# Attention and a gated feed-forward on one core: masks and residual additions moved from GpSimd to VectorE, output matmuls given a later priority

## The chip, the cores and the metric

The kernel runs on one core of a Trainium2 chip. The metric is device time in microseconds of one execution, the median of the runs made. A core has five engines that run their own instruction queues in order: TensorE (PE in the rows, its weight loads PEld), VectorE (DVE), ScalarE (ACT), GpSimd (POOL) and SyncE (SP). They meet only through semaphores.

## The reference

Four batches of eight heads, 768 positions, 64 channels each. Heads 0, 2 and 6 attend causally to everything; the other five see the first four positions and a window of 64. The 3072 tokens that come out, 512 wide, pass a gated feed-forward with hidden width 1536:

```python
scores = scale * np.matmul(q, k.transpose(0, 1, 3, 2))
stream_keep = causal & (is_sink | in_win)
full_mask = np.broadcast_to(causal, (H, S, S))
mask = np.where(retr[0, :, 0, 0, None, None], full_mask, stream_mask)
scores = np.where(mask[None, :, :, :], scores, -1000000000.0)
a = np.exp(scores)
a = a / (np.sum(a, axis=-1, keepdims=True) + 1e-09)
x = np.matmul(a, v)
...
g = x @ w_gate
gelu = 0.5 * g * (1.0 + erf(g * inv_sqrt2))
val = x @ w_val
ffn_out = gelu * val @ w_out
res_gate = 1.0 / (1.0 + np.exp(-(x @ w_res)))
return x + res_gate * ffn_out
```

## The kernel before

The program is a graph of tasks. Each task names its engine, a guessed duration, the tasks whose data it needs (`deps`), tasks that it merely has to follow (`order`), a priority (`prio`, lower is earlier) and the buffers it uses. `schedule()` plays the graph through once when the kernel is built: whenever an engine is free it takes, among its tasks that are ready and whose buffers are to be had, the one of lowest priority number. Tasks made with `flex` may go to one of several engines, whichever ends first by the guessed durations plus `BIAS`. What comes out is a fixed instruction order for each engine, with semaphore waits added. So a priority decides the order, and nothing is decided at run time.

The tokens come in six chunks of four tiles of 128 (`CHUNKS`); chunks 1 and 4 join two half tiles of two batches and so work with 256 query columns where the others have 512. A chunk c goes through four parts.

- *Loads and transposes.* GpSimd's queue issues the loads of q, k and v (L444) into two staging buffers `qks`. In chunks 0 and 1 TensorE transposes q and k (L524) at priority 1000c - 550; later chunks use transposing DMAs on SP.
- *Attention*, priority 1000c to 1000c + 200: per pair of heads the scores (L621), `exp` on ScalarE (L633) into `er` (causal heads) or `es` (the others), a multiplication by a 0/1 mask (L661; VectorE or GpSimd), the values matmul (L689), whose 65th column gives the sum, a reciprocal (L696) and the normalisation (L699) on VectorE into `xtok`. For every two heads a cast to fp16 (L713; VectorE, ScalarE or GpSimd), TensorE transposes (L719) and copies out of PSUM into `xT` (L726; VectorE or ScalarE).
- *Gate and value*, priority 1000c + 500: for each of twelve blocks of 128 hidden units four gate and four value matmuls of 512 columns (L763), GELU on ScalarE (L770), product on VectorE into `hT` (L772).
- *Outputs*, priority 1000c + 1600: for each of four token tiles four residual-gate matmuls (L788, weights `wr`), twelve output matmuls (L793, weights `wo`), a tanh on ScalarE (L796), the gated product on VectorE (L798), the addition of `xtok` (L801; on GpSimd, in the last chunk on VectorE) and the store through SP (L807).

By these priorities the outputs of chunk c - 1 run among the attention of chunk c: scores and values first, output matmuls where TensorE would wait. The scores of a chunk are held until the gate matmul of the eleventh block of the chunk before (`near_end`). Eight PSUM banks serve all this: two for the values matmuls, six for the rest, of which the feed-forward may hold five (`moe`) and scores and transposes four (`scr`).

Of the kernel before, what the change touches and what calls it, by code (L numbers as in the profile page):

```python
# [38 lines left out]

class Task:  # L40
    __slots__ = ("eng", "dur", "fn", "deps", "order", "prio", "bufs", "fset", "dma",
                 "ndeps", "users", "ready", "end", "done", "pos", "snap", "waits",
                 "signal", "name", "sem", "seq", "grp", "alts")

    def __init__(self, eng, dur, fn, deps, prio, bufs=(), fset=None, dma=0.0, order=(), name="", grp=None):
# [58 lines left out]
BIAS = {"act": 0.2, "dve": 0.5, "pool": 0.0}  # L104
# [254 lines left out]
def build_kernel(nc, q, k, v, w_gate, w_val, w_out, w_res, out):  # L359
# [27 lines left out]
    P_ot = Pool(many("otile", 3, [128, D_MODEL], FP32))  # L387
# [3 lines left out]
    P_ps = Pool(banks[2:8], caps={"moe": 5, "scr": 4})  # L391
# [104 lines left out]
    def loads_rows(c, si, b, a, z):  # L496
# [20 lines left out]
        for p in ORDER:  # L517
            pr = 1000 * c - 550 + p if c else 40 * ORDER.index(p) - 5
# [42 lines left out]
    last_gelu = {-1: None}  # L561
    chunk_xt = {-1: []}
    near_end, last_sc, exps_of = {}, {}, {}

    def attention(c, lt0, b, a, z, xbuf, xtbuf, xtoks, xttoks):
# [3 lines left out]
        for k_, p in enumerate(ORDER):  # L569
            pr = 1000 * c + 40 * k_ + (80 if lt0 else 0)  # L570
            side = []
            for h in PAIRS[p]:
# [4 lines left out]
                else:  # L577
# [14 lines left out]
    def scores(c, BB, p, pr, sides, r):  # L592
# [37 lines left out]
    def exps(c, pr, S_, blocks, scr, ts):  # L630
# [9 lines left out]
        while i < len(blocks):  # L640
# [23 lines left out]
            tm = G.flex({"dve": (c_dve(w * 128, 1.4, False), fm), "pool": (c_pool(w * 128, 0.55), fm)}, [tx, mt], pr,  # L664
# [43 lines left out]
    def to_features(c, lt0, n, cb, pr, normed, xbuf, xtbuf, xttoks):  # L708
        x16 = Buf(P_x16)
        def cast(on):  # L710
            def fn(e):
# [172 lines left out]
```

## Time and profile before

| | us |
|---|---|
| runs | 305.07, 309.48, 305.82 |
| median | 305.82 |
| profiled execution | 304.34 |
| its span (first to last instruction) | 302.3 |
| TensorE busy | 279.0 |
| ScalarE busy | 162.1 |
| VectorE busy | 143.3 |
| GpSimd busy | 136.8 |
| mean granted clock of TensorE | 0.989 |

The trace is of one execution. Busy time of an engine counts its computing instructions; issuing a DMA shows as busy on GpSimd's row where its duration is told. The window view gives each engine's busy time in a stretch and the share of full clock that TensorE was granted there; the timeline gives instructions with the idle time just before them and what ended it, in square brackets; the chain follows the work that ended last back to its releasers.

### The profile page before, as it was taken

Reading aid. Unit: us, or ns where it says so; the run is one execution under the profiler, and the core shown is the slowest. Engines: PE = TensorE matmul, PEld = TensorE weight load, DVE = VectorE, ACT = ScalarE, POOL = GpSimd, SP = SyncE. Lnnn points to the kernel's source line nnn. Section 1 sums busy time; section 2 is a strip of 40 time slices with the busy share of each in tenths; the row PEclk is TensorE's granted clock in tenths of the full one; section 3 lists DMA queues with packets and bytes.
Section 4 is the critical chain, followed back from the end, with each engine's and each line's share of the span. In section 5 each row is a group of like instructions: output and inputs, shape, how many; then the busy total and the mean of one; then the engine's idle time right before and its main releaser. Section 6 shows DMA issues by size and latency. Waiting matters only on the chain.

```text
span 302.3 us, 5444 instructions
## 1 busy us (share of the span) xinstructions
PE 279.0 (92%) x2162; PEld 136.3 (45%) x2162; DVE 143.3 (47%) x332; ACT 162.1 (54%) x305; POOL 136.8 (45%) x179
## 2 busy tenths in 40 slices
PE   5986799998489999989999999999999999989994
PEld 5653344454234435534445444445444345444441
DVE  6564334368734324743446443237843315633333
ACT  2896444766143577743376733565643667743310
POOL 8999099686948356680016300347700025400000
PEclk9999999999699999999999999999999999999999
DMA  8999999999999978999301100010100001000011
GB/s 88 184 198 204 174 201 194 158 150 139 153 192 204 104 78 85 85 161 174 61 1 40 67 2 0 18 54 15 58 35 2 0 35 37 37 35 0 2 70 69
DMA packets 92265, 26.94 MB, mean 89 GB/s; under 512 B 81152, under 2 KB 88912, under 8 KB 92240
## 3 DMA queue, kind: packets, MB, share of 16 engines
q0 software_dynamic: 70320, 14.69, 57.9%
q1 hardware_dynamic: 21920, 11.91, 19.3%
q8 instruction: 17, 0.28, 0.4%
q14 instruction: 8, 0.07, 0.1%
HBM read 29.36 MB, written 6.29 MB: 118 GB/s over the span
## 4 chain that ended last, share of the span: by engine, by line
PE 81%; DMA 6%; DVE 5%; POOL 5%; ACT 1%; issue 1%; POOLq 0%; DVEq 0%
PE pb L763 38%; PE pb L793 21%; PE pb L621 7%; PE pb L788 7%; DMA qks<-in_q_dram 6%; PE pb L689 4%; PE pb L719 2%; DVE es L661 1%; POOL va L444 1%; ACT xT L726 1%; POOL qks L444 1%; DVE x L713 1%; DVE xtok L699 1%; PE pb L524 1%; POOL wg L444 1%
## 5 line engine op out<-in xcount | busy, mean ns | idle before, releaser
L763 PE MATMUL pb<-xT,wg 128*128 128x512 f16 x288 | 86.3, 381 | 3.5 <-ACT xT L726 2.5
L772 DVE SCALAR_TENSOR_TENSOR hT<-gact,pb 128x512 f16<-128x512 f16 x72 | 49.5, 687 | 77.2 <-ACT gact L770 77.2
L763 PE MATMUL pb<-xT,wv 128*128 128x512 f16 x288 | 85.6, 383 | 0.2 <-DMA wv<-in_moe_w_val_dram 0.2
L770 ACT ACTIVATE gact<-pb 128x512 f16<-128x512 f32 x72 | 43.0, 597 | 68.8 <-PE pb L763 68.8
L793 PE MATMUL pb<-wo,hT 128*128 128x512 f16 x288 | 73.2, 380 | 0.0
L801 POOL TENSOR_TENSOR otile<-otile,xtok 128x512 f32<-128x512 f32 x20 | 25.4, 1273 | 67.9 <-DVE otile L798 65.4
L763 PEld LDWEIGHTS pb<-xT,wv 128*128 128x128 f16 x288 | 27.8, 98 | 33.2 <-issue 0.6
L763 PEld LDWEIGHTS pb<-xT,wg 128*128 128x128 f16 x288 | 26.3, 98 | 35.0 <-ACT xT L726 4.6
L633 ACT ACTIVATE er<-pb 128x512 f16<-128x512 f32 (+2 forms) x72 | 34.9, 548 | 9.4 <-PE pb L621 9.3
L633 ACT ACTIVATE es<-pb 128x512 f16<-128x512 f32 (+1 forms) x60 | 31.0, 568 | 10.9 <-PE pb L621 9.4
L793 PEld LDWEIGHTS pb<-wo,hT 128*128 128x128 f16 x288 | 23.9, 97 | 25.2 <-issue 2.1
L444 POOL DMA_DIRECT2D qks<-in_k_dram x36 | 28.4, 816 | 13.4 <-PE pb L524 8.6
L798 DVE SCALAR_TENSOR_TENSOR otile<-srs,pb 128x512 f32<-128x512 f32 x24 | 16.4, 684 | 32.6 <-PE pb L793 22.7
L621 PE MATMUL pb<-qkt 64*128 64x128 f16 (+6 forms) x416 | 30.1, 244 | 0.0
L444 POOL DMA_DIRECT2D qks<-in_q_dram x36 | 28.4, 820 | 0.3 <-POOL ident L415 0.3
L661 POOL TENSOR_TENSOR es<-es,m_diag 128x256 f16<-128x256 f16 (+1 forms) x14 | 11.9, 858 | 29.8 <-ACT es L633 29.8
L788 PE MATMUL pb<-wr,xT 128*128 128x512 f16 x96 | 24.7, 380 | 0.0
L444 POOL DMA_DIRECT2D va<-in_v_dram x24 | 21.5, 933 | 5.2 <-PE pb L689 5.2
L621 PEld LDWEIGHTS pb<-qkt 64*128 64x128 f16 (+1 forms) x416 | 13.9, 97 | 18.2 <-issue 6.2
L699 DVE TENSOR_TENSOR xtok<-pb,rcp 128x256 f32<-128x256 f32 (+1 forms) x64 | 21.4, 350 | 0.7
L696 DVE RECIPROCAL rcp<-pb 128x4 f32<-128x4 f32 (+1 forms) x64 | 10.6, 172 | 23.6 <-PE pb L689 22.7
L796 ACT ACTIVATE srs<-pb 128x512 f32<-128x512 f32 x24 | 14.3, 599 | 10.1 <-PE pb L788 10.1
(52 smaller groups left out, 243.7 us busy)
## 6 DMA issues: line engine op xcount, KB each, us to landing
out_dram<-otile SPq DMA_DIRECT2D x24, 256.0 KB, 2.0
va<-in_v_dram POOLq DMA_DIRECT2D x24, 128.0 KB, 12.0
qks<-in_k_dram POOLq DMA_DIRECT2D x32, 64.0 KB, 10.6
qks<-in_q_dram POOLq DMA_DIRECT2D x32, 64.0 KB, 10.7
wg<-in_moe_w_gate_dram POOLq DMA_DIRECT2D x3, 512.0 KB, 11.8
wv<-in_moe_w_val_dram POOLq DMA_DIRECT2D x3, 512.0 KB, 13.6
wo<-in_moe_w_out_dram POOLq DMA_DIRECT2D x4, 384.0 KB, 24.9
qks<-in_q_dram POOLq DMA_DIRECT2D x4, 256.0 KB, 11.7
```

Of the source, the lines that this page charges most:

```text
L444: return G.add(eng, issue, lambda e: e.dma_start(out_ap(), in_ap), deps, prio, bufs=bufs, dma=cost, name=name, grp=grp)
L621: return [e.matmul(at(scr)[rows, o:o + nq * 128], lhsT=at(BB.qkt)[half, 1, kt, p, ks], rhs=at(BB.qkt)[half, 0, q0:q0 + nq, p, :], start=Tr ...
L633: tx = G.add("act", c_act(cols), lambda e: e.activation(out=at(et)[:, off:off + cols], in_=at(scr)[:, 0:cols], func=AF.Exp, scale=SM_SCALE ...
L661: fm = lambda e, o0=off + o, w=w, msk=msk: e.tensor_tensor(out=at(et)[:, o0:o0 + w * 128].rearrange("p (i k) -> p i k", k=128), in0=at(et) ...
L699: t2 = G.add("dve", c_dve(n * 64), lambda e: e.tensor_tensor(out=at(xbuf)[:, lt0:lt0 + n, h * 64:(h + 1) * 64], in0=at(av)[:, 0:n * 65].re ...
L763: return lambda e: [e.matmul(at(dst)[:, :], lhsT=w[:, ci, f * 128:(f + 1) * 128], rhs=at(xtbuf)[:, ci, :], start=(ci == 0), stop=(ci == NC ...
L770: ta = G.add("act", c_act(512), (lambda gb=gb, ga=ga: lambda e: e.activation(out=at(ga)[:, :], in_=at(gb)[:, :], func=AF.Gelu))(), [tg], p ...
L772: th = G.add("dve", c_dve(512), (lambda vb=vb, ga=ga, f=f: lambda e: e.scalar_tensor_tensor(out=at(h)[:, f, :], in0=at(ga)[:, :], scalar=0 ...
L788: e.matmul(at(rb)[:, :], lhsT=at(xtbuf)[:, ci, s], rhs=wr[:, ci, :], start=(ci == 0), stop=(ci == NCB - 1))
L793: e.matmul(at(fb)[:, :], lhsT=at(h)[:, fi, s], rhs=wo[:, fi, :], start=(fi == 0), stop=(fi == NF - 1))
L798: t1 = G.add("dve", c_dve(512), (lambda fb=fb, sr=sr, ot=ot: lambda e: e.scalar_tensor_tensor(out=at(ot)[:, :], in0=at(sr)[:, :], scalar=1 ...
L801: fa = lambda e, ot=ot, lt=lt: e.tensor_tensor(out=at(ot)[:, :], in0=at(ot)[:, :], in1=at(xbuf)[:, lt, :], op=ALU.add)
```

## The change

Masks are `add`ed on VectorE alone; casts choose between VectorE and ScalarE; the residual additions are on VectorE in every chunk, at a priority 90 behind the rest of their token tile. So GpSimd computes nothing after the constants and only issues loads. `BIAS` is lowered by 0.2 for ScalarE and 0.3 for VectorE. The transposes of q and k of chunk 1 get a priority of 1000c - 492, which is behind the first eight gate blocks of chunk 0 instead of ahead of all. The outputs go from 1000c + 1600 to 1000c + 2400, behind the gate and value matmuls of the next chunk; but the first half of these (those of the first two channel blocks) is set to 1000c + 1499 until all feature copies of the chunk are done. The residual-gate matmuls must now follow the last value matmul of their chunk. `xtok`, `xT` and `otile` get one buffer more each, and the feed-forward may hold four PSUM banks instead of five. The orderings between chunks are the same ones, gathered in a loop at the end; `SPLIT` is empty, so the branches for part "A" do nothing.

```diff
-BIAS = {"act": 0.2, "dve": 0.5, "pool": 0.0}
+BIAS = {"act": 0.0, "dve": 0.2}
...
                 for t in cand[e]:
+                    if t.boost and all(x.end is not None and x.end <= now for x in t.boost[0]):
+                        t.prio, t.boost = t.boost[1], None
...
-    P_x = Pool(many("xtok", 2, [128, 4, D_MODEL], FP32))
+    P_x = Pool(many("xtok", 3, [128, 4, D_MODEL], FP32))
-    P_xt = Pool(many("xT", 2, [128, NCB, 512], FP16))
+    P_xt = Pool(many("xT", 3, [128, NCB, 512], FP16))
-    P_ot = Pool(many("otile", 3, [128, D_MODEL], FP32))
+    P_ot = Pool(many("otile", 4, [128, D_MODEL], FP32))
-    P_ps = Pool(banks[2:8], caps={"moe": 5, "scr": 4})
+    P_ps = Pool(banks[2:8], caps={"moe": 4, "scr": 4})
...
-            pr = 1000 * c - 550 + p if c else 40 * ORDER.index(p) - 5
+            pr = 1000 * c - 492 + p if c else 40 * ORDER.index(p) - 5
...
-            tm = G.flex({"dve": (c_dve(w * 128, 1.4, False), fm), "pool": (c_pool(w * 128, 0.55), fm)}, [tx, mt], pr,
+            tm = G.add("dve", c_dve(w * 128, 1.4, False), fm, [tx, mt], pr,
                         bufs=[et], name=f"mask{S_.h}")
...
-        tc_ = G.flex({"dve": (c_dve(n * 128, 1.2, False), cast("dve")), "act": (c_act(n * 128), cast("act")),
-                      "pool": (c_pool(n * 128), cast("pool"))},
+        tc_ = G.flex({"dve": (c_dve(n * 128, 1.2, False), cast("dve")), "act": (c_act(n * 128), cast("act"))},
...
+                if c0 == 0 and c > 0:
+                    for t in (tg, tv):
+                        t.boost, t.prio = ([t_ for _, t_ in xttoks], pr), 1000 * c + 1499
...
-            pr = 1000 * c + 1600 + 10 * lt
+            pr = 1000 * c + 2400 + 10 * lt
...
-                for ci in range(NCB)])(), [t for _, t in xttoks] + [wtok["r"]], pr, bufs=[rb, xtbuf], name="res")
+                for ci in range(NCB)])(), [t for _, t in xttoks] + [wtok["r"]], pr, bufs=[rb, xtbuf],
+                       order=[ph(c, "gv")[-1][1]], name="res")
...
-            alts = {"dve": (0.69, fa)} if c == len(CHUNKS) - 1 else {"pool": (1.3, fa)}
-            t2 = G.flex(alts, [t1] + xtoks[lt], pr, bufs=[ot, xbuf], name="add")
+            t2 = G.add("dve", 0.69, fa, [t1] + xtoks[lt], pr + (0 if c == len(CHUNKS) - 1 else 90), bufs=[ot, xbuf], name="add")
...
+    for c in range(len(CHUNKS)):
+        gv, gelu = ph(c, "gv"), ph(c, "gelu")
+        for f, t in gv:
+            t.order += ph(c, "scA") + ph(c, "scB")
...
+        for t in ph(c + 1, "scB"):
+            t.order += [x for f, x in gv if f == NF - 2] + ph(c, "xT")
+        for t in ph(c + 1, "expB"):
+            t.order += gelu[NF - 1:]
```

The first place is GpSimd during the attention of chunk 1. Before, masks, a cast and additions stand between the loads of q (`in_q_dram`), k and v:

```order
L661 TENSOR_TENSOR es<-es,m_diag 128x256
L661 TENSOR_TENSOR es<-es,m_prev 128x256
L444 DMA qks<-in_k_dram 128x4x64
L713 CAST x<-xtok 128x256
L444 DMA qks<-in_q_dram 128x4x64 x2
L444 DMA qks<-in_k_dram 128x4x64 x2
L444 DMA qks<-in_q_dram 128x4x64 x2
L661 TENSOR_TENSOR es<-es,m_prev 128x128 x2
L444 DMA va<-in_v_dram 128x8x64 x4
L661 TENSOR_TENSOR es<-es,m_diag 128x256
L661 TENSOR_TENSOR es<-es,m_prev 128x128
L801 TENSOR_TENSOR otile<-otile,xtok 128x512 x3
```

Now, at the same loads, nothing but loads:

```order
L451 DMA qks<-in_k_dram 128x4x64 x2
L451 DMA va<-in_v_dram 128x8x64 x4
L451 DMA qks<-in_q_dram 128x4x64 x2
L451 DMA qks<-in_k_dram 128x4x64 x2
L451 DMA qks<-in_q_dram 128x4x64 x2
```

The computing instructions have gone from the queue, and so has everything that a load had to wait behind other than a free buffer.

The second place is VectorE at the end of the attention of chunk 1, up to the first hidden-layer product. Before, with `m_prev`, `m_diag` and `m_causal` the masks, `rcp` the reciprocals:

```order
L661 TENSOR_TENSOR es<-es,m_prev 128x128
L661 TENSOR_TENSOR er<-er,m_causal 128x256
L661 TENSOR_TENSOR es<-es,m_prev 128x128
L696 RECIPROCAL rcp<-pb 128x2
L661 TENSOR_TENSOR es<-es,m_diag 128x256
L699 TENSOR_TENSOR xtok<-pb,rcp 128x2x64
L696 RECIPROCAL rcp<-pb 128x2
L699 TENSOR_TENSOR xtok<-pb,rcp 128x2x64
L696 RECIPROCAL rcp<-pb 128x2
L699 TENSOR_TENSOR xtok<-pb,rcp 128x2x64
L696 RECIPROCAL rcp<-pb 128x2
L699 TENSOR_TENSOR xtok<-pb,rcp 128x2x64
```

Now (L673 is the mask, L708 the reciprocal, L711 the normalisation, L725 the cast, L815 the gated product, L818 the addition in the changed file):

```order
L673 TENSOR_TENSOR es<-es,m_diag 128x256
L673 TENSOR_TENSOR es<-es,m_prev 128x128
L673 TENSOR_TENSOR es<-es,m_diag 128x256
L673 TENSOR_TENSOR es<-es,m_prev 128x128
L708 RECIPROCAL rcp<-pb 128x2
L815 SCALAR_TENSOR_TENSOR otile<-srs,pb 128x512
L711 TENSOR_TENSOR xtok<-pb,rcp 128x2x64
L708 RECIPROCAL rcp<-pb 128x2
L725 CAST x<-xtok 128x256
L711 TENSOR_TENSOR xtok<-pb,rcp 128x2x64
L815 SCALAR_TENSOR_TENSOR otile<-srs,pb 128x512 x2
L818 TENSOR_TENSOR otile<-otile,xtok 128x512 x3
```

Four masks stand together, three gated products and a cast stand among the last reciprocals and normalisations, and three additions follow at the end, behind all attention work of the chunk. Chunk 4 has the same rows in the changed kernel.

The third place is TensorE in the gate and value stretch of chunk 0. Before, the transposes of chunk 1's q and k (L524) begin after 28 gate and value matmuls:

```order
L763 MATMUL pb<-xT,wv 128x512 x2
L763 MATMUL pb<-xT,wg 128x512 x2
L763 MATMUL pb<-xT,wv 128x512 x2
L524 MATMUL pb<-ident,qks 64x128 x12
L763 MATMUL pb<-xT,wg 128x512 x2
L524 MATMUL pb<-ident,qks 64x128 x4
L763 MATMUL pb<-xT,wv 128x512 x2
L524 MATMUL pb<-ident,qks 64x128 x16
L763 MATMUL pb<-xT,wg 128x512 x2
```

Now they come later, sixteen at a time, each sixteen behind a pair of gate and value blocks (L776 is the gate and value matmul, L531 the transpose in the changed file):

```order
L776 MATMUL pb<-xT,wv 128x512 x2
L776 MATMUL pb<-xT,wg 128x512 x2
L776 MATMUL pb<-xT,wv 128x512 x2
L531 MATMUL pb<-ident,qks 64x128 x16
L776 MATMUL pb<-xT,wg 128x512 x2
L776 MATMUL pb<-xT,wv 128x512 x2
L776 MATMUL pb<-xT,wg 128x512 x2
L776 MATMUL pb<-xT,wv 128x512 x2
L531 MATMUL pb<-ident,qks 64x128 x16
```

Ahead of the first of these transposes stand 64 gate and value matmuls of chunk 0 instead of 28, ahead of the last sixteen 88 instead of 40.

## Rows read from the trace of the kernel before

**Rows 1.** Page, part 1: span, then busy time, share and instructions of each engine.
```profile
span 302.3 us, 5444 instructions
PE 279.0 (92%) x2162; PEld 136.3 (45%) x2162; DVE 143.3 (47%) x332; ACT 162.1 (54%) x305; POOL 136.8 (45%) x179
```

**Rows 2.** Windows: length, busy PE, PEld, DVE, ACT, POOL (count), PEclk, DMA, GB/s.
```profile
51.70:84.67 32.97, 27.01 (x240) 13.11 (x241) 20.15 (x61) 19.33 (x40) 26.53 (x36) 0.90 1.96 151
103.84:131.57 27.73, 26.35 (x256) 12.92 (x257) 13.13 (x36) 20.77 (x39) 18.39 (x23) 1.00 0.84 88
150.31:171.14 20.83, 20.43 (x203) 10.41 (x203) 11.53 (x30) 16.10 (x32) 8.29 (x9) 1.00 0.07 26
190.53:218.67 28.14, 27.49 (x253) 13.68 (x251) 16.47 (x54) 17.88 (x36) 16.87 (x24) 1.00 0.10 39
238.04:265.64 27.60, 26.28 (x257) 12.91 (x257) 12.19 (x32) 20.28 (x38) 10.24 (x9) 1.00 0.08 30
```

**Rows 3.** Chain that ended last: start us, us, what; 86 gate and value matmuls.
```profile
219.31 18.73 PE pb L763 x86
```

**Rows 4.** Windows at chunk 1's end, columns as in rows 2.
```profile
74.50:80.10 5.60, 0.86 (x8) 0.28 (x9) 5.57 (x7) 0.77 (x2) 5.60 (x7) 0.74 1.96 154
80.10:84.70 4.60, 3.65 (x17) 1.49 (x18) 1.18 (x5) 1.60 (x4) 4.60 (x7) 0.57 1.69 159
```

**Rows 5.** Timeline there: start us, us, engine, line, what [idle before <-releaser].
```profile
75.58 2.88 DVE L661 TENSOR_TENSOR es<-es,m_prev 128x128 f16<-128x128 f16 x1
...
75.91 3.69 POOL L801 TENSOR_TENSOR otile<-otile,xtok 128x512 f32<-128x512 f32 x3
...
80.09 0.21 PE L689 MATMUL pb<-va,es 128*128 128x65 f16 x1 [3.68 <-DVE rcp L696]
...
82.08 1.06 PE L763 MATMUL pb<-xT,wv 128*128 128x512 f16 x2
```

**Rows 6.** VectorE durations: timeline, groups (busy us, mean ns), one line (ns min/median/max).
```profile
66.39 0.28 DVE L661 TENSOR_TENSOR es<-es,m_diag 128x256 f16<-128x256 f16 x1
...
210.50 0.21 DVE L661 TENSOR_TENSOR es<-es,m_prev 128x128 f16<-128x128 f16 x1
...
L696 DVE RECIPROCAL rcp<-pb 128x2 f32<-128x2 f32 x32 | 5.0, 166 | 11.0 <-PE pb L689 10.6
L699 DVE TENSOR_TENSOR xtok<-pb,rcp 128x128 f32<-128x128 f32 x32 | 8.7, 285 | 0.3
L798 DVE SCALAR_TENSOR_TENSOR otile<-srs,pb 128x512 f32<-128x512 f32 x24 | 16.4, 684 | 32.6 <-PE pb L793 22.7 <-ACT srs L796 9.7
L801 DVE TENSOR_TENSOR otile<-otile,xtok 128x512 f32<-128x512 f32 x4 | 2.8, 692 | 0.1
L713 DVE CAST x<-xtok 128x256 f16<-128x256 f32 x4 | 2.8, 702 | 0.0
L726 DVE COPY xT<-pb 128x256 f16<-128x256 f16 x5 | 1.4, 285 | 0.7 <-PE pb L719 0.5
...
L713 DVE CAST x<-xtok x5: 395/565/1052, 71.7 to 217.4; 128x256 f16<-128x256 f32 x4, 128x512 f16<-128x512 f32 x1
```

**Rows 7.** Chunk 0's gate stretch: timeline of PE, then rows of the chain.
```profile
27.51 0.60 PE L763 MATMUL pb<-xT,wg 128*128 128x512 f16 x2 [0.69 <-ACT xT L726]
...
33.46 0.53 PE L524 MATMUL pb<-ident,qks 128*64 128x128 f16 x12 [1.89 <-DMA qks<-in_q_dram]
...
15.47 17.94 DMA qks<-in_q_dram
...
38.92 0.57 PE pb L524 x16
```

**Rows 8.** wo's loads (issue ns, first and last start; median landing), first output matmul.
```profile
L444 POOL DMA_DIRECT2D wo<-in_moe_w_out_dram x4: 860/872/888, 23.1 to 25.4; - x4
...
wo<-in_moe_w_out_dram POOLq DMA_DIRECT2D x4, 384.0 KB, 24.9
...
L793 PE MATMUL pb<-wo,hT x288: 377/379/390, 53.0 to 297.8; 128*128 128x512 f16 x144
```

More of the change, by code (lines that the diff above doesn't have):

```diff
@@ L37 @@
 ROWS_UNTIL = 2
+SPLIT = {c: (6, ((0, 0), (1, 0), (2, 0), (3, 0)) if len(CHUNKS[c]) > 1 else ((0, 0), (2, 0))) for c in ()}
 class Task:
@@ L51, in __init__ @@
         self.ready = 0.0
+        self.end = None
         self.done = None
@@ L57, in __init__ @@
         self.alts = None
+        self.boost = None
 class Buf:
@@ L559, in loads_natural, with ph, part @@
                 values(b, a, z, base, False)
-    last_gelu = {-1: None}
-    chunk_xt = {-1: []}
-    near_end, last_sc, exps_of = {}, {}, {}
+    phase = {}
+    def ph(c, part):
+        return phase.setdefault((c, part), [])
+    def part(c, p, late):
+        return "A" if c in SPLIT and (p, late) in SPLIT[c][1] else "B"
     def attention(c, lt0, b, a, z, xbuf, xtbuf, xtoks, xttoks):
@@ L581, in attention @@
                     h, Buf(P_er if IS_RETRIEVAL[h] else P_es), pack(diag, rest), {}, {}, 0
+                S_.part = part(c, p, int(lt0 > 0))
                 side.append(S_)
@@ L623, in sc @@
                     for (_, _, half, scr, rows, (kt, ks), o, q0, nq) in mms]
-        ts = G.add("pe", c_mm(128, dur), sc, deps, pr, bufs=scrs + [BB.qkt], order=chunk_xt[c - 1] + [near_end.get(c - 1)],
-                   name=f"sc{p}")
-        last_sc.setdefault(c, []).append(ts)
+        ts = G.add("pe", c_mm(128, dur), sc, deps, pr, bufs=scrs + [BB.qkt], name=f"sc{p}")
+        ph(c, "sc" + S_.part).append(ts)
         for (x, S_), scr in zip(sides, scrs):
@@ L755, in gate_value @@
         toks = []
-        G.add("act", 0.2, lambda e: e.activation(out=scratch[:, :], in_=ident[:, 0:1], func=AF.Gelu), [t_ident],
-              1000 * c - 100, fset="gelu", order=exps_of[c], name="table")
+        for part_ in ("B", "A") if c + 1 in SPLIT else ("B",):
+            ph(c, "table" + part_).append(G.add(
+                "act", 0.2, lambda e: e.activation(out=scratch[:, :], in_=ident[:, 0:1], func=AF.Gelu), [t_ident],
+                1000 * c - 100 + (600 if part_ == "A" else 0), fset="gelu", name="table"))
         for f in range(NF):
@@ L827, in build_kernel @@
         output(c, h, htoks, xbuf, xtoks, xtbuf, xttoks)
+    for c in range(len(CHUNKS)):
+        gv, gelu = ph(c, "gv"), ph(c, "gelu")
+        for f, t in gv:
+            t.order += ph(c, "scA") + ph(c, "scB")
+        for t in ph(c, "tableB"):
+            t.order += ph(c, "expA") + ph(c, "expB")
+        if c + 1 == len(CHUNKS):
+            continue
+        m = SPLIT[c + 1][0] if c + 1 in SPLIT else NF
+        for t in ph(c + 1, "scB"):
+            t.order += [x for f, x in gv if f == NF - 2] + ph(c, "xT")
+        for t in ph(c + 1, "expB"):
+            t.order += gelu[NF - 1:]
+        for t in ph(c + 1, "scA"):
+            t.order += [x for f, x in gv if f == m - 2] + ph(c, "xT")
+        for t in ph(c + 1, "expA"):
+            t.order += gelu[m - 1:m]
+        for t in ph(c, "tableA"):
+            t.order += ph(c + 1, "expA")
+        for f, t in gv:
+            if f >= m:
+                t.order += ph(c + 1, "scA")
+        for f in range(m, NF):
+            gelu[f].order += ph(c + 1, "expA")
     span = G.schedule()
```

18 lines of the change are left out of this document (9 added, 9 removed).

## Prediction

> **What bounds the kernel now.** Read the page's engine line first [rows 1]: TensorE is busy 279.0 of 302.3 us, no other engine above 162, so the end is set by TensorE, and a change can win only where TensorE waits, or lose by making it wait. The profiled execution took 304.34 us, 2.04 more than its span; the three timed runs have a median of 305.82. I sum changes against the profiled execution and put them on the median, which is what will be compared.
>
> Next comes the table by stretch [rows 2]: the five stretches in which attention of chunk 1 to 5 runs with the outputs of the chunk before, each from the end of the gate matmuls before it to the first gate matmul that no attention work interrupts. Subtract TensorE's busy time from each length. Chunks 2 to 5 leave 1.4, 0.4, 0.7 and 1.3 us idle. Chunk 1 leaves 6.0 idle, and its granted clock is 0.90. Chunks 1 and 4 have the same tiles, so they are each other's yardstick: chunk 4 took 28.14, of which about 2.6 are twelve output matmuls that stand only here, ahead of its first score (12 times the 0.218 of [rows 3], 18.73 us for 86), hence 25.5. Chunk 1 took 32.97, that is 7.4 more for the same work.
>
> Where those 7.4 go is seen at chunk 1's end [rows 4, 5]. From 74.5 to 80.1 TensorE is busy 0.86 of 5.6 us, while VectorE and GpSimd are both busy throughout. A VectorE mask of 128x128 takes 2.88 us; such a mask takes 0.21 elsewhere [rows 6]. Beside it run three GpSimd residual additions, 3.69 us, and it ends when they are nearly done. The values matmul behind it starts at 80.09 after 3.68 idle. After this pause the clock is granted at 0.57 up to 84.7, and a pair of 512-column matmuls takes 1.06 us instead of 0.60 [rows 7]: the array is partly at 1.2 instead of 2.4 GHz.
>
> The other large wait is in chunk 0's gate and value stretch [rows 7]: the transposes of chunk 1's q and k stand in TensorE's order ahead of the data. TensorE idles 1.89 us at 33.46 for the q load, which landed after a 17.94 us transfer. The first score of chunk 1 is at 51.70 [rows 2].
>
> **The change, step by step.** Read from the order of instructions, since the planner decides it.
>
> *Chunk 0's stretch.* The first q and k transposes now stand behind 64 gate and value matmuls instead of 28, eight of these ahead of the stretch and 56 in it. From 27.51 to 51.70 are 24.2 us; the work in it is 86 of 96 gate and value matmuls (18.7 us) and 64 transposes in four times about 0.55 (2.2), 20.9 in all, so 3.3 are waits. In the changed order 88 matmuls are left (19.2), with the transposes 21.4; these start 56 times 0.218, or 12.2 us, after the stretch begins, about 39, when the old kernel ran its last transposes unhindered (38.92). Also the last two feature copies, which ScalarE made one after the other so that TensorE idled 0.69 at 27.51, are now split between ScalarE and VectorE: the stretch starts some 0.6 sooner, about 26.9. I add 0.4 for PSUM banks, as each new block of 16 transposes needs four at once. The first score then comes at 26.9 + 21.4 + 0.4 = 48.7: **-3.0**. Bounds: -2.0 (1 us more of bank waits) to -3.6.
>
> *Chunk 1.* GpSimd has no additions, masks or casts left; the collision of [rows 5] cannot occur, and the stretch becomes that of chunk 4, whose new order it shares row by row. Its price is therefore that of chunk 4 after the change.
>
> *Chunk 4.* VectorE receives 14 masks, four additions and three casts here. Counting its new instructions in the stretch and multiplying by [rows 6]: 21 masks of 256 columns at 0.28, five of 128 at 0.21, 16 reciprocals at 0.166, 16 normalisations at 0.285, four gated products at 0.684, four additions at 0.692, five casts at 0.702, three copies at 0.285: 24.0 us, where it was busy 16.5 of 28.14. If none of this reaches TensorE the stretch can lose at most its idle time, -0.7; if all that is added does, +7.5. What decides is the end: four masks now stand as a block right ahead of the last two heads' values matmuls, 0.98 us, and a gated product between the last reciprocal and its normalisation, which chunk 4 had before too. Against that, the masks meet no GpSimd work any more. Nearest is the old chunk 4, with work of the same kind: I take **+0.5**, hence 25.5 + 0.5 = 26.0 for both, and for chunk 1 32.97 - 26.0 = **-6.9** (bounds -7.4 to 0).
>
> Casts may still collide with the issue of loads, which stays on GpSimd: five VectorE casts of before took 395 to 1052 ns, the widest of them the shortest [rows 6]. If each of five in the stretch were held for one whole issue of 0.87 [rows 8], 4.4 us, of which 0.3 each is in the 0.702 already, VectorE would have 2.9 more to do; that is part of the second rival. [...]
>
> *Chunk 3.* Only here are output matmuls really held back: the last twelve move from behind the gate stretch to between the last values matmuls and the last transposes, where they cover normalisation and cast. TensorE idles 0.4 in this stretch: **-0.3** (bounds -0.4 to +1.0, if masks queue on VectorE).
>
> *Chunks 2 and 5.* The last transposes and the first gate matmuls keep nearly their order, and the chain from the last values matmul over VectorE, cast and copy stays: **0** each (-0.7 to +1.5). The additions now stand ahead of the hidden-layer products of the next stretch; four take 2.8 us [rows 6], while GELU has still to give the first product its input, and what the products feed are output matmuls that come behind all gate matmuls, 18.7 us [rows 3]. One fewer PSUM bank for the feed-forward is covered: two feature blocks alternate over four banks, a bank is needed again two blocks later.
>
> *Loads.* Queued alone, they start when staging is free. Chunk 1's transposes end near 48 instead of 39.5 [rows 7], so chunk 2's loads start some 8 us later, but chunk 2's scores are 45 us away then, and a load took 18. The tail behind the last gate matmul keeps its order. Both at 0.
>
> Sum: -3.0 - 6.9 + 0.5 - 0.3 = -9.7; 305.82 - 9.7 = **296.1**, and a profiled execution of about 294.6.
>
> **Rivals.**
> 1. *As above*, with each term near its value: 292 to 299.5, **62 in 100**.
> 2. *VectorE becomes the bound of chunks 1 and 4.* For it: 24.0 us of instructions against 25.5 us, in order, with reciprocals that wait for TensorE between them. Against: consecutive instructions overlap a little, and in old chunk 4 masks met GpSimd's, so that part of its 16.5 was waiting. With half of the 7.5 on the path in both, 3.8 instead of 0.5 each, and 0.7 more in chunks 2, 3 and 5: -9.7 + 6.6 + 2.1 = -1.0, so 304.8. **15 in 100.**
> 3. *The slower side: the clock falls at the end of chunks 1 and 4.* If VectorE's block of masks, gated product and casts leaves TensorE a pause like the 3.68 us of [rows 5], the clock follows and both stretches cost what chunk 1 cost: no gain in chunk 1, +7.4 in chunk 4: -3.0 + 7.4 - 0.3 = +4.1, or 309.9. It decides from a pause of that length on; I count at most about 1.5 us in one piece (0.98 of masks, and a cast with its latency). **6 in 100.** The Trainium skill, "TensorE: Matmul & The Clock Gate" (What's actually happening), calls the slow clock the default, which activity lifts; the 0.57 behind the pause agrees.
> 4. *Chunk 0's gain is given back.* TensorE reaches the first output matmul, at 53.0 before, 3 us sooner; the last of its four weight loads is issued at 25.4, and the four land 24.9 later in the median, so near 50.3 or somewhat after [rows 8]. If all of the first term is lost there, 299.1. Against: that quarter is wanted by the last three of twelve matmuls only, 2 us behind the first, and loads may land sooner where GpSimd does nothing else. **11 in 100.**
> 5. *More than forecast*, if chunk 4 also loses its idle time and chunks 2 and 5 some of theirs: -9.7 - 2.4 = -12.1, 293.7 or less; below 292 **6 in 100.**
>
> **How the numbers follow.** The likeliest case gives 296.1. The range leaves out case 3, half of case 2 and most of what is below 292: 292 to 303.5. About 2% (6.1 us, to 299.7) is what a measurement of this kernel can tell from no change. Faster by more: case 1, case 5 and a little of case 4, **0.69**; within: most of 2 and 4, part of 3, **0.26**; slower (over 311.9): **0.05**.
>
> **What would show it.** First score of chunk 1 near 48.7 and no TensorE wait for a q load; chunk 1's stretch near 26 with clock 1.00; no mask over 0.5 us; chunk 4's near 26. Wrong if TensorE's waits there end on VectorE masks, or the clock dips in either.

## Result, and the profile after

| | before | after |
|---|---|---|
| median of the runs, us | 306.47 | 296.47 |
| ratio to before | | 0.965, 95% interval 0.9554 to 0.9746 |
| profiled execution, us | 304.34 | 295.47 |
| its span, us | 302.3 | 293.6 |

Timed again on another chip beside two other kernels (below), the changed kernel took 298.46 against 306.27, a ratio of 0.9725 (0.9667 to 0.9784). Executions more than 1.5% above the fastest of their kernel are left out of the ratios. The change is worth 8 to 10 us.

The page's engine line of the changed kernel, to be held against [rows 1]:

```profile
span 293.6 us, 5444 instructions
PE 278.1 (95%) x2162; PEld 137.6 (47%) x2162; DVE 152.3 (52%) x393; ACT 160.0 (55%) x301; POOL 86.5 (29%) x122
```

TensorE's busy time hardly moved (279.0 to 278.1): what went is its waiting. VectorE has 61 instructions more and is busy 9 us longer, GpSimd 57 fewer and 50 us less.

From here on "chunk c takes" means the time from the last gate or value matmul of chunk c - 1 to that of chunk c, so that the same work is counted whatever the order in it. One row is one chunk, from 0 to 5; columns as in [rows 2]. Before:

```profile
0.00:51.53 51.53, 42.13 (x456) 24.46 (x456) 25.19 (x54) 29.17 (x60) 41.89 (x64) 1.00 1.42 178
51.53:103.68 52.15, 46.19 (x329) 21.73 (x328) 28.32 (x73) 26.30 (x52) 36.56 (x48) 0.93 1.93 164
103.68:150.15 46.47, 45.09 (x343) 21.34 (x342) 20.69 (x47) 27.73 (x51) 22.17 (x26) 1.00 1.06 105
150.15:190.37 40.22, 39.77 (x292) 19.00 (x292) 19.09 (x41) 23.66 (x44) 9.02 (x9) 1.00 0.06 21
190.37:237.88 47.51, 46.82 (x341) 22.21 (x339) 24.03 (x65) 25.22 (x49) 16.87 (x24) 1.00 0.08 29
237.88:284.22 46.34, 45.02 (x344) 21.43 (x344) 19.75 (x43) 27.25 (x50) 10.24 (x9) 1.00 0.06 24
```

After:

```profile
0.00:48.57 48.57, 42.96 (x456) 25.73 (x456) 25.18 (x55) 28.41 (x59) 29.84 (x49) 1.00 1.41 181
48.57:94.61 46.04, 44.66 (x329) 21.16 (x328) 25.86 (x86) 25.55 (x50) 33.51 (x45) 1.00 2.03 158
94.61:140.92 46.31, 44.82 (x343) 21.42 (x342) 23.18 (x52) 27.32 (x50) 23.15 (x30) 1.00 1.52 140
140.92:183.21 42.29, 42.23 (x303) 20.50 (x302) 23.04 (x53) 23.13 (x43) 0.00 (x0) 1.00 0.07 26
183.21:229.25 46.04, 44.66 (x329) 21.12 (x328) 25.70 (x86) 25.55 (x50) 0.00 (x0) 1.00 0.06 24
229.25:275.56 46.31, 44.82 (x344) 21.52 (x344) 23.18 (x52) 27.32 (x50) 0.00 (x0) 1.00 0.06 24
```

The first column of numbers is the length. Chunk 0 ends 2.96 us sooner; chunk 1 takes 6.11 less, at a granted clock of 1.00 instead of 0.93; chunk 2, 0.16 less. Twelve output matmuls (2.59 us, by 12 times 0.216) moved from chunk 4's row into chunk 3's; without them chunk 3 takes 0.5 less and chunk 4 1.1 more. Chunk 5 and the tail stay. That is the whole difference of the spans, 8.7.

Chunk 4's end after the change, where [rows 5] showed chunk 1's end before; start, us, engine, line, what, and in brackets the idle time before and what ended it (chunk 1's end has the same rows, with idle times of 0.78, 0.17 and 0.36 too). The names of the lines are those of the changed file: L673 mask, L701 values, L711 normalisation, L725 cast, L730 transpose, L815 gated product.

```profile
206.50 0.28 DVE L673 TENSOR_TENSOR es<-es,m_diag 128x256 f16<-128x256 f16 x1
...
206.84 0.20 PE L701 MATMUL pb<-va,es 128*128 128x65 f16 x1 [0.78 <-DVE es L673]
...
207.33 0.67 DVE L815 SCALAR_TENSOR_TENSOR otile<-srs,pb 128x512 f32<-128x512 f32 x1
207.92 0.28 DVE L711 TENSOR_TENSOR xtok<-pb,rcp 128x128 f32<-128x128 f32 x1
...
208.59 0.28 PE L730 MATMUL pb<-ident,x 128*128 128x128 f16 x2 [0.17 <-DVE x L725]
209.23 0.29 PE L730 MATMUL pb<-ident,x 128*128 128x128 f16 x2 [0.36 <-ACT x L725]
```

The mask of 128x256 takes 0.28 us, and none of that size takes more than 0.29 in the whole kernel. The waits that are left end on the block of four masks and on the last two casts.

### The profile page after: what moved, and what is told of

Its sections match the earlier page's. It is cut to its first block, busy times and chain, and to the rows that moved or that the text cites. A ratio compares the mean times of both kernels' runs of the same rounds, so it can differ in the third digit from the quotient of the medians.

```text
span 293.6 us, 5444 instructions
## 1 busy us (share of the span) xinstructions
PE 278.1 (95%) x2162; PEld 137.6 (47%) x2162; DVE 152.3 (52%) x393; ACT 160.0 (55%) x301; POOL 86.5 (29%) x122
## 4 chain that ended last, share of the span: by engine, by line
PE 90%; DVE 4%; ACT 3%; issue 1%; POOL 0%; POOLq 0%; DVEq 0%
PE pb L776 41%; PE pb L810 23%; PE pb L634 8%; PE pb L804 7%; PE pb L701 5%; PE pb L827 3%; PE pb L531 2%; PE pb L730 2%; ACT x L725 1%; DVE xtok L711 1%; DVE es L673 1%; DVE otile L815 1%; ACT xT L737 1%; ACT es L645 1%; DVE rcp L708 0%
## 5 line engine op out<-in xcount | busy, mean ns | idle before, releaser
L776 PE MATMUL pb<-xT,wg 128*128 128x512 f16 x288 | 85.2, 379 | 2.3 <-ACT xT L737 2.3
L776 PE MATMUL pb<-xT,wv 128*128 128x512 f16 x288 | 85.2, 379 | 0.0
L776 PEld LDWEIGHTS pb<-xT,wv 128*128 128x128 f16 x288 | 28.0, 98 | 33.3 <-issue 0.2
L776 PEld LDWEIGHTS pb<-xT,wg 128*128 128x128 f16 x288 | 27.1, 98 | 33.7 <-DVE otile L818 1.8
L815 DVE SCALAR_TENSOR_TENSOR otile<-srs,pb 128x512 f32<-128x512 f32 x24 | 16.2, 682 | 24.3 <-PE pb L810 19.1
L708 DVE RECIPROCAL rcp<-pb 128x4 f32<-128x4 f32 (+1 forms) x64 | 10.1, 172 | 25.3 <-PE pb L701 24.8
L711 DVE TENSOR_TENSOR xtok<-pb,rcp 128x256 f32<-128x256 f32 (+1 forms) x64 | 20.9, 349 | 0.3
L818 DVE TENSOR_TENSOR otile<-otile,xtok 128x512 f32<-128x512 f32 x24 | 16.1, 686 | 0.3
L701 PE MATMUL pb<-va,es 128*128 128x65 f16 x120 | 13.3, 195 | 1.7 <-DVE es L673 1.6
```

The source lines that it names most:

```text
L701: r.append(e.matmul(at(av)[:, (i - a) * 65:(i - a) * 65 + 65], lhsT=at(et)[:, pos:pos + 128], rhs=val, start=(i == a and y == 0), stop=(y ...
L711: t2 = G.add("dve", c_dve(n * 64), lambda e: e.tensor_tensor(out=at(xbuf)[:, lt0:lt0 + n, h * 64:(h + 1) * 64], in0=at(av)[:, 0:n * 65].re ...
L776: return lambda e: [e.matmul(at(dst)[:, :], lhsT=w[:, ci, f * 128:(f + 1) * 128], rhs=at(xtbuf)[:, ci, :], start=(ci == 0), stop=(ci == NC ...
L815: t1 = G.add("dve", c_dve(512), (lambda fb=fb, sr=sr, ot=ot: lambda e: e.scalar_tensor_tensor(out=at(ot)[:, :], in0=at(sr)[:, :], scalar=1 ...
L818: fa = lambda e, ot=ot, lt=lt: e.tensor_tensor(out=at(ot)[:, :], in0=at(ot)[:, :], in1=at(xbuf)[:, lt, :], op=ALU.add)
```

## The experiments

What the planner makes of single edits undone is seen in the order of instructions. Without the third buffers of `xtok` and `xT` and the fourth of `otile`, and without the residual gate's new ordering, the order of every engine is the same row for row; with the outputs at 1600 again, that of TensorE, VectorE, ScalarE and GpSimd is. These three edits are idle, the later priority of the output matmuls in the title among them. Chunk 3's twelve output matmuls move by another edit: without the priority 1499 for the first half of the gate and value matmuls they stay where they were. That edit, the four PSUM banks and `BIAS` do change the order, and none of the three was run alone. The experiments are about the transposes' priority, the masks, the additions and the collision itself.

**One number alone, and the additions or masks alone.** Each starts from the kernel before:

```diff
# b_qkt, b_qkt_t
-            pr = 1000 * c - 550 + p if c else 40 * ORDER.index(p) - 5
+            pr = 1000 * c - 492 + p if c else 40 * ORDER.index(p) - 5
# b_adds
-            alts = {"dve": (0.69, fa)} if c == len(CHUNKS) - 1 else {"pool": (1.3, fa)}
-            t2 = G.flex(alts, [t1] + xtoks[lt], pr, bufs=[ot, xbuf], name="add")
+            t2 = G.add("dve", 0.69, fa, [t1] + xtoks[lt], pr + (0 if c == len(CHUNKS) - 1 else 90), bufs=[ot, xbuf], name="add")
# b_masks
-            tm = G.flex({"dve": (c_dve(w * 128, 1.4, False), fm), "pool": (c_pool(w * 128, 0.55), fm)}, [tx, mt], pr,
+            tm = G.add("dve", c_dve(w * 128, 1.4, False), fm, [tx, mt], pr,
```

> The kernel before with one edit: the transposes of chunk 1's q and k at priority 1000c - 492 instead of 1000c - 550. My theory, that they waited for loads and only need to stand later: the last gate or value matmul of chunk 0 ends near 49.2 instead of 51.53 us (the changed kernel reached 48.57, of which 0.6 came from splitting the two feature copies, which is not done here), no wait of TensorE for a q load, and the whole execution is some 2.4 us shorter, chunk 1's attention being as slow as before. Rival, that the loads came in time only because GpSimd had nothing else to do: a wait for q of 1 us or more stays and chunk 0 ends after 50.5.

Measured: 297.16 us in one execution, beside 307.05 for the kernel before. Neither theory had this: with one number changed, and masks and additions still free to go to GpSimd, chunk 1 took 46.15 us instead of 52.15, with the clock at 1.00. Chunk 0 ended at 49.90 here, near the 49.2 of my theory, and at 54.14 in the second profile of this kernel. The row of chunk 1:

```profile
49.90:96.05 46.15, 44.61 (x329) 20.89 (x328) 23.33 (x80) 26.21 (x52) 39.10 (x50) 1.00 2.02 168
```

GpSimd's timeline in that stretch tells why:

```profile
48.41 1.50 POOL L444 DMA_DIRECT2D qks<-in_k_dram  x2 [18.54 <-PE pb L524]
...
63.07 1.66 POOL L444 DMA_DIRECT2D qks<-in_k_dram  x2
69.75 3.52 POOL L444 DMA_DIRECT2D va<-in_v_dram  x4 [5.02 <-PE pb L689]
...
79.08 1.59 POOL L444 DMA_DIRECT2D qks<-in_q_dram  x2
80.57 3.83 POOL L801 TENSOR_TENSOR otile<-otile,xtok 128x512 f32<-128x512 f32 x3
```

Chunk 2's loads wait for the staging buffers that chunk 1's transposes (L524) empty. With the transposes later, the loads run through chunk 1's attention, from 48.4 to 80.6; the planner finds GpSimd taken (in its planned times loads stand there without a gap), puts all masks on VectorE, and the three additions come at 80.57, behind the attention. In the kernel before, these loads started at 38.37, ten microseconds sooner, GpSimd had time to spare from 57 on, and got masks and additions to do:

```profile
38.37 1.50 POOL L444 DMA_DIRECT2D qks<-in_k_dram  x2 [8.61 <-PE pb L524]
...
55.95 0.95 POOL L444 DMA_DIRECT2D qks<-in_k_dram  x1
59.70 0.77 POOL L661 TENSOR_TENSOR es<-es,m_diag 128x256 f16<-128x256 f16 x1 [2.79 <-ACT es L633]
```

So the one number removes the collision by keeping GpSimd busy.

> The kernel before with the residual additions of all chunks on VectorE, 90 behind in priority; masks still go to VectorE or GpSimd. Chunk 1's time, from the last gate or value matmul of chunk 0 to that of chunk 1, was 52.15 us before and 46.04 in the changed kernel. My theory, that the three additions beside a VectorE mask made the 3.68 us pause and the slow clock behind it: chunk 1 falls to 47 to 48, no VectorE mask above 1.4 us, granted clock 1.00 there. Rival, that the masks on GpSimd and its load issues are the cause: chunk 1 stays above 50.

Measured: chunk 1 took 46.88 us at a clock of 1.00; the longest VectorE mask in it 0.755. The theory holds: without the three additions the pause and the slow clock are gone, although masks stay on GpSimd. The whole execution still took 307.90, because its chunk 0 took 57.65 us; more on that below.

> The kernel before with all masks on VectorE; the additions stay on GpSimd. My theory, that an addition on GpSimd holds up a VectorE mask that runs into it: masks of 1 us or more are still seen wherever an addition runs beside them, and chunk 1 gains less than the 6.1 us of the changed kernel, ending between 47 and 51 (52.15 before). Rival, that GpSimd's masks were what hurt: chunk 1 falls to 46 to 46.5 and no mask is above 0.6.

Measured: 306.73 us in one execution. Chunk 1 took 50.97 us at a clock of 0.93, which is within the theory's range but not by its mechanism. One mask in it took 1.22 us, and what lay beside that one was the issue of loads; the one mask of the chunk that ran into an addition took 0.50 instead of 0.28. (In later chunks of this run masks beside additions took up to 1.49 us.) The largest wait of TensorE was for a cast (one row of TensorE, one of GpSimd):

```profile
78.85 0.39 PE L719 MATMUL pb<-ident,x 128*128 128x128 f16 x2 [2.30 <-POOL x L713]
...
78.35 0.44 POOL L713 CAST x<-xtok 128x256 f16<-128x256 f32 x1
```

One of the last casts had gone to GpSimd and stood there behind load issues until 78.35. So a cast on GpSimd can be late at the end of this chunk too, not the additions only.

**Both in turn, timed.** The changed kernel with the old number, beside the other two on one chip:

```diff
# a_qkt550 (from the changed kernel)
-            pr = 1000 * c - 492 + p if c else 40 * ORDER.index(p) - 5
+            pr = 1000 * c - 550 + p if c else 40 * ORDER.index(p) - 5
```

> The kernel before with the transposes of chunk 1's q and k at 1000c - 492, timed. In its profile chunk 0's loads and transposes end later, so chunk 2's loads occupy GpSimd's queue during chunk 1's attention and the planner puts chunk 1's masks on VectorE and the additions behind the attention. Theory A, that this one number brings most of the gain: a ratio to the kernel before of 0.970 to 0.976 (297 to 299 against 306.5), and the changed kernel at most 2.5 us faster than it. Theory B, that chunk 0's part in the single look was luck: 0.98 or more.

> The changed kernel with the transposes of chunk 1's q and k back at 1000c - 550. Theory A (two separate causes for chunk 1, each enough by itself): chunk 1 keeps its 46.0 us, since GpSimd computes nothing; only chunk 0's part is lost, its last gate or value matmul ends near 51.5 instead of 48.6, so 298 to 300 in all, 0.972 to 0.98. Rival, that the later loads are what saves chunk 1: chunk 1 takes 50 us or more, 303 and above.

> The changed kernel as it is, timed beside the others on the same chip. Both theories: 0.963 to 0.969 of the kernel before (295.5 to 297).

| kernel | median, us | ratio to before (95%) | chunk 1, us |
|---|---|---|---|
| before | 306.27 | 1 | 52.15 (its profile on the first chip) |
| number alone (b_qkt_t) | 299.13 | 0.9781 (0.9726 to 0.9836) | 46.15 |
| all of the change but the number (a_qkt550) | 299.03 | 0.9756 (0.9706 to 0.9806) | 46.10 |
| both (after_t) | 298.46 | 0.9725 (0.9667 to 0.9784) | 46.04 |

Each half alone brings chunk 1 to the same 46.1 us and the kernel to 299; together they bring 0.6 us more, which these intervals can't tell from nothing. So theory A was right on chunk 1 (two causes, each enough by itself). The ratios expected of the number alone (0.970 to 0.976) and of both (0.963 to 0.969) were too good.

**Additions back on GpSimd in the changed kernel.**

```diff
# a_adds_pool (from the changed kernel)
-            t2 = G.add("dve", 0.69, fa, [t1] + xtoks[lt], pr + (0 if c == len(CHUNKS) - 1 else 90), bufs=[ot, xbuf], name="add")
+            t2 = G.add(*(("dve", 0.69) if c == len(CHUNKS) - 1 else ("pool", 1.3)), fa, [t1] + xtoks[lt],
+                       pr + (0 if c == len(CHUNKS) - 1 else 90), bufs=[ot, xbuf], name="add")
```

> The changed kernel with the residual additions of chunks 0 to 4 back on GpSimd at their late priority; masks and casts stay on VectorE and ScalarE. My theory: masks beside an addition are stretched again to 1 us or more, in chunk 1 and in chunk 4, and chunks 1 and 4 take 1 to 4 us longer each than 46.04, so 297 to 303 in all against 295.5. Rival, that moving the masks alone was enough and additions at the late priority come behind all masks: chunks 1 and 4 stay within 0.5 us of 46.04 and VectorE's relief of 0.69 us for each addition makes the kernel up to 1 us faster.

Measured: 304.04 us in one execution. The place was wrong: chunks 1 and 4 took 45.72 and 46.39, chunk 2 took 50.21 instead of 46.31. There two additions ran into the masks:

```profile
119.80 2.91 POOL L818 TENSOR_TENSOR otile<-otile,xtok 128x512 f32<-128x512 f32 x2
...
120.12 1.47 DVE L673 TENSOR_TENSOR er<-er,m_causal 128x512 f16<-128x512 f16 x1
121.52 1.48 DVE L673 TENSOR_TENSOR es<-es,m_prev 128x512 f16<-128x512 f16 x1
...
121.65 0.54 PE L701 MATMUL pb<-va,er 128*128 128x65 f16 x12 [1.57 <-DVE er L673]
```

Masks of 512 columns take about 0.42 in the changed kernel; here each took the length of an addition, and TensorE idled 1.57 us for one. Behind this the clock was at 0.50 to 0.84 up to 128 us. Not all of it is the additions': the mask ahead of these two took 1.90 us with the issue of loads beside it. Without chunk 0 this execution took 248.35 us against 245.02 of the changed kernel, 3.3 more. Chunks 1 and 5 were 0.3 and 0.6 shorter, as the rival had it of VectorE's relief.

**The collision by itself.** Extra work on GpSimd that nobody waits for, behind the last exp of chunk 4, where the changed kernel's GpSimd does nothing. All other engines keep their order but for one fill at the start.

```diff
# a_dum_add (and a_dum_set2 with range(6) and e.memset(dum[1][:, :], 0.0)); both with the old numbers of buffers of xtok, xT, otile, to make room
+    dum = [sb(f"dum{i}", [128, 512], FP32) for i in range(2)]
+    td = G.add("dve", 0.4, lambda e: e.memset(dum[0][:, :], 1.0), [], -93, name="dum0")
+    for _ in range(3):
+        td = G.add("pool", 1.3, lambda e: e.tensor_tensor(out=dum[1][:, :], in0=dum[0][:, :], in1=dum[0][:, :], op=ALU.add),
+                   [td, ph(4, "expB")[-1]], 5900, name="dum")
```

> The changed kernel (with the three buffer pools of before, which leaves the order as it is) and, on GpSimd, three extra additions of 128x512 fp32 on tiles that nothing else uses, behind the last exp of chunk 4: work that only collides. The order of all other engines is that of the changed kernel. Theory, that a VectorE mask is held by a GpSimd instruction that reads SBUF: VectorE masks of 1 to 3 us at the end of chunk 4, a pause of TensorE there of 1.5 to 3.5 us, a granted clock below 0.9 behind it if the pause is above 3 us, and chunk 4 takes 48 to 53 us instead of 46.04, while chunk 1 stays at 46.0. Rival, that the additions cost because others wait for their results: nothing changes, chunk 4 stays within 0.3 us of 46.04.

Timeline of a_dum_add at chunk 4's end, then its window by chunk:

```profile
207.19 3.49 POOL L874 TENSOR_TENSOR dum<-dum 128x512 f32<-128x512 f32 x3 [79.79 <-ACT es L645]
...
209.70 1.13 DVE L673 TENSOR_TENSOR es<-es,m_diag 128x256 f16<-128x256 f16 x1
...
210.88 0.20 PE L701 MATMUL pb<-va,es 128*128 128x65 f16 x1 [0.81 <-DVE es L673]
...
186.06:234.56 48.50, 46.39 (x329) 21.58 (x328) 27.08 (x86) 25.55 (x50) 3.33 (x3) 0.96 0.06 23
```

> As a_dum_add, but GpSimd's extra work behind the last exp of chunk 4 is six fills of 128x512 fp32 with a constant, which read no SBUF. Theory, that the collision needs GpSimd to read SBUF: VectorE masks at the end of chunk 4 stay at 0.2 to 0.3 us, chunk 4 takes 46.0 to 47.7 us (the changed kernel gave 46.04 and 47.69 in two profiles, the second with a spell of 1.2 GHz). Rival, that any GpSimd instruction on SBUF holds a two-input VectorE instruction: a mask of 1 us or more as in a_dum_add, and a second pause of TensorE of 0.8 us or more.

The same place with the fills:

```profile
208.00 3.48 POOL L874 MEMSET dum<- 128x512 f32 x6 [79.76 <-ACT es L645]
...
208.30 0.98 DVE L725 CAST x<-xtok 128x256 f16<-128x256 f32 x2
...
210.53 0.28 DVE L673 TENSOR_TENSOR es<-es,m_diag 128x256 f16<-128x256 f16 x1
...
186.90:232.94 46.04, 44.67 (x329) 21.16 (x328) 26.07 (x86) 25.55 (x50) 3.20 (x6) 1.00 0.06 24
```

As long on GpSimd, 3.5 us, and as idle for everybody else: beside additions one mask took 1.13 instead of 0.28 and TensorE had one more pause, of 0.81; beside fills the masks, TensorE's pauses and the 46.04 us are those of the changed kernel. What collides here is a VectorE mask, which has two SBUF inputs, and a GpSimd operation that reads SBUF. So it is not only through semaphores that the engines meet, other than was said at the start. The Trainium skill, "SBUF — State Buffer" (Who interferes with whom), says that a VectorE instruction with two SBUF inputs contends with a GpSimd instruction that reads SBUF, not with one that only writes it; for the masks both runs agree.

Two things don't fit into this pair. Casts were held by the fills too: two took 0.37 and 0.69 us beside them, where 0.28 is usual (one took 0.92 beside the additions); TensorE didn't wait for them. And three masks were stretched with only the issue of loads beside them: 1.22 us in b_masks, 1.35 and 1.90 in a_adds_pool. In the changed kernel 43 masks lay so, and none was longer than usual (0.43 at most, of 512 columns). Why those three were is open.

The pause was smaller than expected (0.81, not 1.5 to 3.5), since only one of the four masks was held. Of the 2.46 us that chunk 4 lost, 0.81 is the pause; the rest is a spell of 1.2 GHz behind it (clock 0.96 in the row), which after_t shows in its chunk 4 too, without any extra work (47.69 us). So the spell is not put down to the additions.

**Two attempts at a faster kernel.** Both from the changed kernel:

```diff
# a_warm160, a_wl
-    for _ in range(90):
+    for _ in range(160):
# a_lat0, a_wl
-                    lat = 0.0 if u.eng == e and not t.dma and e == "pe" else LAT[e]
+                    lat = 0.0 if not t.dma and (u.eng == e and e == "pe" or t.name == "rcp") else LAT[e]
```

> The changed kernel with 160 instead of 90 filler matmuls (their results are never read): the extra 70 land where the planner sees TensorE idle in chunk 0's attention, among them 32 around the last two blocks of transposes ahead of chunk 0's gate matmuls; all other rows keep their order. Theory, that the spread of 5 us between executions of the changed kernel is chunk 0, where pauses of TensorE between 14 and 28 us are followed by 1.2 GHz in some executions: chunk 0 ends at 48.5 to 49.5 us with a granted clock above 0.97 from 20 us on, the spread shrinks to about 2 us, and the median falls to 295 to 296.5 against 298.5 for the changed kernel on the chip before this (0.965 to 0.968 of the kernel before). Rival, that chunk 0 varies because its loads land at different times: spread and median stay as they were, 0.970 to 0.975.

Measured: 297.31 us, a ratio of 0.9701 (0.9646 to 0.9756), the same as the changed kernel within the intervals. The theory failed: the spread did not shrink (296.35 to 302.30), and in the profiled execution, the longest of the six, the clock was 0.62 from 20 to 28 us and chunk 0 ended at 55.40. The mean granted clock of the six was 0.986 to 1.000, that of the changed kernel 0.982 to 1.000 in its ten, so the fillers are not shown to hold the clock. In a_wl, which has the same fillers and another order, the granted clock was 1.00 from 12 us to chunk 0's end, and it still ended at 50.64, 2 us later than in the best profile without them.

> The kernel with 160 filler matmuls, and a planner that thinks that a normalisation can follow its reciprocal without latency, so that no gated product is put between the two. Theory, that in chunks 1 and 4 the gated product of 0.67 us between the last reciprocals and normalisations delays cast and transposes: these chunks take 45.2 to 45.7 us instead of 46.04, the others stay within 0.3. Rival, that the order around it decides: the planner's other choices change with it (the last transposes now stand directly behind the last values matmuls, with no gate matmuls between), and chunks 1 and 4 get longer, 46.3 to 47.5.

Measured: 296.70 us in one execution; chunks 1 and 4 took 46.07 us. Both guesses were wrong there. But chunks 2, 3 and 5 took 45.99, 41.84 and 45.99, 0.3 to 0.45 less each; what in their order brings that was not followed further.

> The changed kernel with 90 filler matmuls as it has, and only the planner's latency between reciprocal and normalisation set to nothing. From the profile of a_wl, chunks 2, 3 and 5 take 45.99, 41.84 and 45.99 us instead of 46.31, 42.29 and 46.31, chunks 1 and 4 stay: 1.0 us less. Chunk 0 spreads as before. So 0.966 to 0.972 of the kernel before, a median 0 to 2 us below the changed kernel's 298.5 on the chip where it was timed, which these rounds can hardly tell from nothing; the stretches of the profile are the measure.

Measured: 296.02 us, a ratio of 0.9649 (0.9594 to 0.9703), against 0.965 and 0.9725 for the changed kernel on its two chips. Chunks 1 to 5 of its profile took 46.06, 45.99, 41.84, 46.06 and 45.99, together 1.05 less than in the changed kernel, as expected. That microsecond is seen in the profiles only: the timed intervals overlap.

## Why the prediction came out as it did

The forecast was 9.7 us less; the medians gave 10.0 less on the first chip and 7.8 on the second, the two profiled executions 8.9. The sum was right, in part by luck, with these terms:

| term | forecast | profile |
|---|---|---|
| chunk 0's stretch | -3.0 | -2.96, but see below |
| chunk 1 | -6.9 | -6.11 |
| chunk 4 | +0.5 | +1.1 |
| chunk 3 | -0.3 | -0.5 |
| chunks 2 and 5, tail | 0 | -0.2 |

*Chunk 0: right in the pair of profiles, not shown as a gain.* The gate stretch began at 26.88 (forecast 26.9), the first score of chunk 1 came at 48.66 (48.7), no wait for q is left. But the ends of chunk 0 in further profiles are: with the transposes early, 51.53, 51.02, 57.65 and 54.06 (before, b_masks, b_adds, a_qkt550); with TensorE's new order in chunk 0, 48.57, 51.59, 51.41, 52.26 and 53.83 (after, after_t, a_dum_add, a_dum_set2, a_adds_pool). One order spreads over 5 us there, more than the term, and of the four with early transposes only the first has a wait of TensorE for chunk 1's q. What goes with the spread is seen in the window from 20 to 28 us, in b_adds first, then in the changed kernel:

```profile
20.00:28.00 8.00, 8.00 (x58) 4.12 (x57) 4.17 (x14) 6.97 (x14) 8.00 (x11) 0.50 1.24 206
...
20.00:28.00 8.00, 5.88 (x68) 3.37 (x68) 4.28 (x15) 6.49 (x13) 8.00 (x11) 1.00 1.24 205
```

In b_adds TensorE had idled before it for a copy into `vs`:

```profile
18.93 0.24 PE L689 MATMUL pb<-vs,es 128*128 128x65 f16 x1 [2.38 <-DMA vs<-va]
```

Behind this it ran at 1.2 GHz until past 27 us and did 58 matmuls in the window where the changed kernel did 68. In the five profiles with the new order the clock in this window was 1.00, 0.79, 0.66, 0.60 and 0.57, as listed. The step that failed is the comparison itself: I summed chunk 0 from one execution as if it were fixed. That -2.96 came out where -3.0 was forecast is luck. Timed, undoing the number costs 0.6 us (a_qkt550 against after_t), not 3.

*Chunk 1: mechanism right, price right, attribution incomplete.* The collision is real (a_dum_add against a_dum_set2), and without the additions on GpSimd 5.3 us of chunk 1's 6.1 are won (b_adds). The stretch up to the first gate matmul that nothing interrupts took 26.17, forecast 26.0; 0.9 us of the gain was lost (4 times 0.218) because four fewer gate and value matmuls fit into it, which my yardstick didn't count. What I did not see is that the later transposes would have removed the collision without moving a single mask by rule. The step is the one on loads: "chunk 2's loads start some 8 us later" was right (47.08 against 38.37), and priced at 0, when its effect on the planner was worth as much as the main term.

*Chunk 4: size off by 0.6.* The two waits named are there (0.78 for the block of masks; 0.17 and 0.36 for casts), together 1.3 in place of 0.47 and 0.18 before, and the four matmuls outside count here too. Before:

```profile
216.26 0.20 PE L689 MATMUL pb<-va,es 128*128 128x65 f16 x1 [0.47 <-DVE xtok L699]
...
218.55 0.28 PE L719 MATMUL pb<-ident,x 128*128 128x128 f16 x2 [0.18 <-DVE x L713]
```

TensorE's waits there do end on VectorE masks, which the prediction had named as a sign of being wrong; at 0.78 us this wait is far from the 3.8 that rival 2 put on the path. VectorE was nowhere near a bound, so rival 2 falls: with 72 instructions it was busy 15.88 us in the stretch where I had counted 24.0, and 54 took 16.47 before:

```profile
183.21:209.38 26.17, 24.79 (x238) 12.23 (x237) 15.88 (x72) 18.30 (x37) 0.00 (x0) 1.00 0.03 12
...
L725 DVE CAST x<-xtok 128x256 f16<-128x256 f32 x10 | 3.0, 319 | 0.0
```

Three things were wrong in the count. A cast takes 0.32 on average, not 0.702. Of the four casts of that size in [rows 6] the longest, 1.05, lay beside an addition on GpSimd, not beside load issues; the other three, 0.51 to 0.68, did lie beside the issue of loads. In the changed kernel one of ten is still held so, at 0.62 in chunk 1, and the rest take 0.28 to 0.29. Three of the four additions, 2.1 us, come behind the stretch. And a mask of 0.28 is followed by the next after 0.20 ([rows 6] give durations, not distances), so a sum of durations counts the overlap twice.

*Rival 3 has a weaker form.* I tied it to a pause like the 3.68 us of [rows 5]. In after_t pauses of 0.78, 0.17 and 0.36 within three microseconds were followed by 1.2 GHz:

```profile
213.24:214.74 1.50, 1.50 (x5) 0.61 (x4) 1.50 (x3) 0.00 (x0) 0.00 (x0) 0.50 0.20 79
```

Chunk 4 took 47.69 there and 46.04 in the first profile, with the same pauses. Chunk 3's gain has its row (idle 0.06 instead of 0.45).

*Rivals 4 and 5 fall in the profile.* The first output matmuls started at 50.08, and the other six of their tile followed among other work, with no wait for `wo`, so nothing was given back there:

```profile
50.08 1.46 PE L810 MATMUL pb<-wo,hT 128*128 128x512 f16 x6
```

And chunk 4 lost time instead of winning some, while chunk 5 stayed.

## What to carry to other kernels

Before an edit is given a gain, ask which other edit of the same change would remove the same wait: two that do are worth one. A residual addition that a slow, idle engine takes for nothing is not free if it reads SBUF beside another engine's two-input operation on the path. And a term that lies in the start of a kernel, if it spreads as chunk 0 does here, should be read from several executions before it enters a sum.

## What the runs showed of the hardware that was not expected

- GpSimd's additions hold up a VectorE mask (0.28 to 1.13 us for 256 columns), its fills of the same total length do not. Casts were held by both (0.92 and 0.69 instead of 0.28).
- The same program, with the same pauses of TensorE, was granted 2.4 GHz in one execution and 1.2 GHz for some 3 us in another (chunk 4: 46.04 and 47.69 us). The Trainium skill, "TensorE: Matmul & The Clock Gate" (What's actually happening), says that the moment of the change varies between executions of the same kernel; these two profiles differ so, and in one of them there is no change in chunk 4 at all.
- Chunks 2 and 5 of the changed kernel took 46.30 or 46.31 us in every profile with its order, chunk 3 42.29 or 42.30: there an execution repeats itself to 0.01 us, chunk 2 with loads beside it too, so single profiles can tell tenths there.
